# Attention scores from two full-height products a head, and all batches in half units

## The chip, the cores and the metric

The kernel runs on one core of a Trainium2 chip. Its engines work side by side, each on its own list of instructions in a fixed order: TensorE (PE, with its weight loads as PEld), VectorE (DVE), ScalarE (ACT), GpSimd (POOL), and SyncE (SP), which here issues all DMAs. Time is device microseconds (us) of one launch, the median of several runs; a profiled execution stands beside it.

## The reference

A small attention with a memory term feeds a two-layer network:

```python
scores = (q @ k.T) / sqrt(D)          # B, H, S, D = 4, 8, 576, 64, causal
local = softmax(scores) @ v
q_p = where(q > 0, q, exp(q) - 1) + 1
mem_out = (q_p @ M_prev) / (q_p @ z_prev + 1e-6)
x = g * mem_out + (1 - g) * local     # g = sigmoid(beta), per head
out = square(relu(x.reshape(2304, 512) @ w_in)) @ w_out     # 512 -> 2048 -> 512
```

All of it is fp32. Products that need more than TensorE's fast fp32 form (fp32r) holds are built from a high part, rounded to fp32r, and a low part, the remainder.

## The kernel before

The network's 2304 tokens go in nine blocks of 256. A block costs 192 `up` products of 256 columns (lines 624 to 626: four contraction slices by 16 slices of the hidden layer, three high/low terms each) and 96 `oacc` products of 512 columns (lines 614 to 616). Block 0 holds the first 64 tokens of the four batches. Each batch then gives two blocks: its query tiles 1 and 2 (the low half), and its tiles 3 and 4 (the high half). A block can start once all four head pairs of its batch have written their half of `x` to `xd` and `prefetch` has read it back as `xn` and transposed it into `px` (lines 588 and 591).

Attention goes in units (b, p, tiles): a batch, a pair of heads, and the query tiles worked on. `SEG = 2` makes half units of batches 0 and 1 (lo and hi, `[1, 2]` and `[3, 4]`) and whole units of batches 2 and 3, so 16 half units (0 to 15) and 8 whole ones (16 to 23). Units 0 to 5 (`NES`) use fp32 directly for the scores and are not split. From unit 6 on, q and k are split: `qh` and `kh` by ACT (lines 359 and 364), `ql` by DVE (line 360), `kl` by POOL in units below 12 (`NEARLY`) and by DVE from there (line 365). One DMA brings k (`kd`), one or two bring q with the memory matrix (`qm`), one brings v (`vv`); `kd` and `vv` have one buffer.

Scores of a tile stand at line 461. The two heads of a pair lie on partitions 0 to 63 and 64 to 127, so each product contracts over 64 rows. A pass is one stretch of keys of one query tile: three terms (high by high, low by high, high by low), each for both heads, six products. Tiles 1, 2 and 3 have one pass of 192, 320 and 448 columns, tile 4 has two of 288. Line 465 (DVE) takes each pass out of PSUM, and the one PSUM buffer `s` is free after that. ACT takes the exponential, `a` is formed in two 16-bit parts, a DMA transposes it into `aT`, and lines 541 to 546 multiply by v. Each unit also scales v once: a maximum over `vv` (line 393, DVE), a broadcast on TensorE (`vt`, line 397), four small DVE steps (lines 395 to 403), and two 16-bit parts (lines 408 on ACT, 410 on DVE).

The order on each engine is set by a scheduler that simulates the program: network products fill TensorE's list where attention, which has to wait for other engines, leaves room. Once made, an engine's order is fixed; an instruction that waits holds up all behind it on its engine.

Of the kernel before, what the change touches and what calls it, by code (L numbers as in the profile page):

```python
# [21 lines left out]
P = 128  # L22
# [37 lines left out]
NEARLY = 12  # L60
SEG = 2
TORD = [2, 1, 3, 4]
# [25 lines left out]
def fused_kernel(ctx: ExitStack, tc: tile.TileContext, t0_d, zt_d, kk_d, qv_d, beta, w_in, w_out, out):  # L88
# [32 lines left out]
    def gates():  # L121
# [10 lines left out]
        nc.vector.tensor_scalar(out=g1b, in0=gpb, scalar1=-1.0, scalar2=1.0, op0=ALU.mult, op1=ALU.add)  # L132

    mask0 = cp.tile([P, D], F32, name="mask0")
    nc.vector.tensor_copy(mask0[:D], mask[:D, 448 : 448 + D])
    nc.vector.tensor_copy(mask0[D:], mask[D:, 512 : 512 + D])

# [84 lines left out]
    def first_tokens(tp, ahead):  # L222
        me, ze, se, xe, ye = ([nc.gpsimd if c == "p" else nc.vector for c in t] for t in TE)
        xh = mo.tile([P, NK, BLK], F32R, tag="xh", name="xh", bufs=2)
        xl = mo.tile([P, NK, BLK], F32R, tag="xl", name="xl", bufs=2)
        xq.append((xh, xl))
        ng = B // GB
        bc = [P, GN, D]
# [4 lines left out]
        for step in SEQ.split():  # L233
            if step == "r":
                ahead()
            elif step == "l":
                nxt.append(loads(*order[0]))
            elif step == "g":
# [90 lines left out]

    def loads(b, p, tiles):  # L330
        qa, qb = QT[tiles[0]][0], sum(QT[tiles[-1]])
        kd = at.tile([P, S], F32, tag="kd", name="kd", bufs=KB)
        nc.sync.dma_start(kd[:, :qb], kk_d[b, p, :, :qb])
        qm = at.tile([P, 2 * ZW + SQ], F32, tag="qm", name="qm", bufs=QB)
        qa, qb = qa - D + 2 * ZW, qb - D + 2 * ZW
        for c0, c1 in [(0, qb)] if qa == 2 * ZW else [(0, 2 * ZW), (qa, qb)]:
            nc.sync.dma_start(qm[:, c0:c1], qv_d[b, p, :, c0:c1])
        vv = at.tile([P, 5 * P], F32, tag="vv", name="vv", bufs=VVB)
        nv = (tiles[-1] + 1) * P
        nc.sync.dma_start(vv[:, :nv], qv_d[b, p, :, SQ + 2 * ZW : SQ + 2 * ZW + nv])  # L340
        return kd, qm, vv

    def attention(b, p, tiles, ld, after, early, sfull, full):
# [5 lines left out]
        qa, qb = QT[tiles[0]][0] - D, kn - D  # L349
        kd, qm, vv = ld  # L350
        q_raw = qm[:, 2 * ZW :]
# [4 lines left out]
        if not sfull:  # L356
            qh, ql = (at.tile([P, SQ], F32R, tag=t, name=t) for t in ("qh", "ql"))
            kh, kl = (at.tile([P, S], F32R, tag=t, name=t) for t in ("kh", "kl"))
            nc.scalar.copy(qh[:, qa:qb], q_raw[:, qa:qb])
            q_eng.tensor_tensor(  # L360
                out=ql[:, qa:qb], in0=q_raw[:, qa:qb], in1=qh[:, qa:qb].bitcast(F32), op=ALU.subtract
            )
            yield
            nc.scalar.copy(kh[:, :kn], kd[:, :kn])
            k_eng.tensor_tensor(out=kl[:, :kn], in0=kd[:, :kn], in1=kh[:, :kn].bitcast(F32), op=ALU.subtract)
            yield
            terms = [(qh, kh), (ql, kh), (qh, kl)]
        else:
            terms = [(q_raw, kd)]

# [76 lines left out]
        for i in [t for t in TORD if t in tiles]:  # L447
# [8 lines left out]
            for s in range(ns):  # L456
                ks = slice(s * w, (s + 1) * w)
                sps = ps.tile([P, 2, 512], F32, tag="s", name="sp")
                for x, (qt, kt) in enumerate(terms):
                    for h, hd in enumerate(heads):  # L460
                        nc.tensor.matmul(  # L461
                            sps[:n, h, :w], qt[hd, qc], kt[hd, ks], start=x == 0, stop=x == len(terms) - 1
                        )
                for h in range(2):
# [236 lines left out]
    if not nxt:  # L701
        nxt.append(loads(*order[0]))

    def attn(i0, i1):
        for i in range(i0, i1):
            ld = nxt.pop()

            def after():
                if i + 1 < len(order):
                    nxt.append(loads(*order[i + 1]))  # L710

            yield from attention(*order[i], ld, after, i < NEARLY, i < NES, i < NEF and max(order[i][2]) < 4)
# [67 lines left out]
```

## Time and profile before

| | before |
|---|---|
| time, median of 3 runs | 610.11 us (610.11 to 610.82) |
| profiled execution | 609.23 us, of which the span is 607.4 us |
| PE busy | 569.1 us (94%) |
| DVE busy | 411.2 us (68%) |
| ACT busy | 329.0 us (54%) |
| POOL busy | 170.3 us (28%) |

The span runs from the first instruction to the last; 1.8 us of the execution lie outside it. A matmul's start in the trace is measured and its end modelled, so matmuls overlap in the list: what a product holds the engine for is read from the distance between starts. Attention ends at about 480 us; behind it only the network runs.

### The profile page before, as it was taken

To read this page: it belongs to the slowest core of one execution; us is meant where nothing else is said; L and a number is where in the kernel's file an instruction comes from. 1 tells how busy PE (TensorE), PEld (TensorE's weight loads), DVE (VectorE), ACT (ScalarE), POOL (GpSimd) and SP (SyncE) were. 2 spreads that over 40 slices of the span, in tenths; PEclk is the share of its full clock that TensorE was granted. 3 is DMA by queue.
4 is the path that set the end of the run, shared out by engine and by line. 5 is a ranking of instruction groups with operands and counts; after the bars stand their busy time and mean duration, and the time that the engine had idled before them with its cause. 6 is when DMAs were issued, how large, how long until landed. Compare 5 with 4: busy or idle time off the path is not lost.

```text
span 607.4 us, 11542 instructions
## 1 busy us (share of the span) xinstructions
PE 569.1 (94%) x4198; PEld 482.7 (79%) x4198; DVE 411.2 (68%) x1285; ACT 329.0 (54%) x747; POOL 170.3 (28%) x139
## 2 busy tenths in 40 slices
PE   2479997999989999999999999999999999999997
PEld 2358876787868787888888888888888899998996
DVE  5999798868677879887888978788697711001000
ACT  3689686756566664775576645654556413312312
POOL 2501232134423233233332233232321121221221
PEclk9989998999997999999999999999999999999999
DMA  8947575673574775664655564575435510100000
GB/s 278 402 144 301 165 210 159 139 169 85 117 165 111 160 155 129 145 173 88 164 115 114 145 126 107 114 167 118 103 70 119 99 24 2 68 1 1 36 1 35
DMA packets 127576, 76.28 MB, mean 126 GB/s; under 512 B 99360, under 2 KB 112672, under 8 KB 127520
## 3 DMA queue, kind: packets, MB, share of 16 engines
q1 hardware_dynamic: 127520, 75.55, 49.7%
q8 instruction: 33, 0.54, 0.4%
q14 instruction: 23, 0.19, 0.1%
HBM read 42.63 MB, written 8.78 MB: 85 GB/s over the span
## 4 chain that ended last, share of the span: by engine, by line
PE 63%; DVE 13%; DMA 9%; ACT 9%; issue 3%; SPq 1%; POOL 1%; ACTq 0%
PE up L624 9%; PE up L626 8%; PE up L625 8%; PE oacc L614 8%; PE oacc L616 8%; PE oacc L615 8%; PE sp L461 6%; DMA aT<-a 3%; DMA vv<-in_qv_dram 3%; ACT e L477 2%; PE acc L546 2%; DVE a L516 2%; PE pm L428 2%; DVE e L465 2%; DVE memx L556 2%
## 5 line engine op out<-in xcount | busy, mean ns | idle before, releaser
L624 PE MATMUL up<-xh,w 128*128 128x256 f32 x576 | 167.0, 290 | 3.4 <-ACT aF L496 2.5
L626 PE MATMUL up<-xh,w 128*128 128x256 f32 x576 | 166.1, 288 | 0.0
L625 PE MATMUL up<-xl,w 128*128 128x256 f32 x576 | 165.9, 288 | 0.0
L639 POOL TENSOR_TENSOR gl<-r,gh 128x512 fp32r<-128x512 f32 x72 | 98.9, 1373 | 203.6 <-DVE gh L638 124.4
L624 PEld LDWEIGHTS up<-xh,w 128*128 128x128 f32 x576 | 111.2, 193 | 10.9 <-issue 3.9
L614 PE MATMUL oacc<-w,gh 128*128 128x512 f32 x288 | 116.0, 403 | 3.6 <-ACT gh L636 3.5
L625 PEld LDWEIGHTS up<-xl,w 128*128 128x128 f32 x576 | 111.3, 193 | 5.2 <-issue 2.5
L615 PE MATMUL oacc<-w,gh 128*128 128x512 f32 x288 | 114.4, 397 | 0.0
L626 PEld LDWEIGHTS up<-xh,w 128*128 128x128 f32 x576 | 111.2, 193 | 3.4 <-issue 2.2
L477 ACT ACTIVATE e<-e,mx 128x320 f32<-128x320 f32 (+3 forms) x128 | 77.8, 609 | 65.4 <-DVE mx L465 65.0
L616 PE MATMUL oacc<-w,gl 128*128 128x512 f32 x288 | 111.7, 403 | 0.0
L516 DVE SCALAR_TENSOR_TENSOR a<-e,a 128x128 f16<-128x128 f32 x120 | 79.4, 677 | 19.8 <-ACT a L514 19.6
L630 ACT ACTIVATE r<-up 128x512 f32<-128x512 f32 x72 | 42.4, 590 | 92.5 <-PE up L626 86.6
L632 POOL TENSOR_TENSOR r<-r 128x512 f32<-128x512 f32 x40 | 46.5, 1162 | 164.1 <-ACT r L630 164.1
L638 DVE CAST gh<-r 128x512 fp32r<-128x512 f32 x40 | 16.9, 423 | 87.9 <-ACT r L634 86.4
L614 PEld LDWEIGHTS oacc<-w,gh 128*128 128x128 f32 x288 | 54.5, 189 | 15.7 <-ACT gh L636 4.0
L616 PEld LDWEIGHTS oacc<-w,gl 128*128 128x128 f32 x288 | 53.2, 189 | 13.5 <-issue 3.8
L465 DVE CUSTOM_DVE_ANT_0 e<-sp,mask 128x320 f32<-128x320 f32 (+3 forms) x128 | 56.2, 475 | 9.0 <-PE sp L461 8.9
L615 PEld LDWEIGHTS oacc<-w,gh 128*128 128x128 f32 x288 | 54.5, 189 | 9.4 <-issue 0.9
L514 ACT ACTIVATE a<-e 128x128 f16<-128x128 f32 x120 | 56.9, 521 | 5.7 <-DMA aT<-a 4.7
L548 DVE TENSOR_REDUCE s<-acc 128x128 f32<-128x256 f32 x60 | 24.0, 417 | 21.2 <-PE acc L546 21.2
L546 PE MATMUL acc<-vs,aT 128*128 128x128 f16 x308 | 37.4, 222 | 0.0
(127 smaller groups left out, 883.4 us busy)
## 6 DMA issues: line engine op xcount, KB each, us to landing
raw<-in_w_in_dram SPq DMA_DIRECT2D x11, 512.0 KB, 7.9
vv<-in_qv_dram SPq DMA_DIRECT2D x16, 320.0 KB, 2.8
raw<-in_w_out_dram SPq DMA_DIRECT2D x9, 512.0 KB, 7.8
kd<-in_kk_dram SPq DMA_DIRECT2D x16, 288.0 KB, 3.1
out_dram<-o SPq DMA_DIRECT2D x16, 256.0 KB, 2.0
xd<-memx SPq DMA_DIRECT2D x31, 128.0 KB, 2.1
xn<-xd SPq DMA_DIRECT2D x14, 256.0 KB, 3.2
qm<-in_qv_dram SPq DMA_DIRECT2D x8, 321.0 KB, 2.9
```

What stands on the lines that cost most here:

```text
L465: nc.vector.tensor_tensor_reduce(out=e[:n, h, ks], in0=sps[:n, h, :w], in1=mask[:n, 448 - q0 + s * w : 448 - q0 + s * w + w], scale=-0.125 ...
L477: nc.scalar.activation(e[:n, h, :ke], e[:n, h, :ke], AF.Exp, bias=bs, scale=-1.0, accum_out=sm[:n, h : h + 1])
L514: nc.scalar.mul(av[:, :, o0 : o0 + w], x, SC)
L516: nc.vector.scalar_tensor_tensor(out=av[:, :, o0 + w : o0 + 2 * w], in0=x, scalar=SC, in1=av[:, :, o0 : o0 + w], op0=ALU.mult, op1=ALU.sub ...
L546: nc.tensor.matmul(o2, aT[:, h * nb + c, :n], vs[:, h, c], start=False, stop=c == i)
L614: nc.tensor.matmul(acc[t], gh[:, u, ts], w_out_op(f, 0), start=f == 0, stop=False)
L615: nc.tensor.matmul(acc[t], gh[:, u, ts], w_out_op(f, 1), start=False, stop=False)
L616: nc.tensor.matmul(acc[t], gl[:, u, ts], w_out_op(f, 0), start=False, stop=f == NF - 1)
L624: nc.tensor.matmul(up[:, u, :], w_in_op(f, k, 0), xh[:, k, :], start=k == 0, stop=False)
L625: nc.tensor.matmul(up[:, u, :], w_in_op(f, k, 0), xl[:, k, :], start=False, stop=False)
L626: nc.tensor.matmul(up[:, u, :], w_in_op(f, k, 1), xh[:, k, :], start=False, stop=k == NK - 1)
L639: nc.gpsimd.tensor_tensor(out=gl, in0=r, in1=gh.bitcast(F32), op=ALU.subtract)
```

## The change

k's high and low part are stacked in one tile: rows 0 to 63 hold the high part of one head's k, rows 64 to 127 its low part, the two heads side by side. For that k is loaded onto both halves of the partitions, ACT rounds all of it, and the lower half is overwritten with the remainder. q is loaded onto both halves too, into a buffer `qd` of its own, and split there into `qh` and `ql`. A product of `qh` with that tile over 128 rows then gives high by high and high by low at once, and one of `ql` adds low by high (and low by low, which the kernel before leaves out). A pass is four products over 128 rows in place of six over 64. The new tiles have room for two query tiles, and `SEG = 4` makes half units of all batches: 32 units, with 16 to 19 and 24 to 27 the low halves of batches 2 and 3. The small `mask0` moves to a pool that is given back early.

```diff
-SEG = 2
+SEG = 4
...
+            kd = at.tile([P, 2, S], F32, tag="kd", name="kd", bufs=KB)
+            qd = at.tile([P, 2, 2 * P], F32, tag="qd", name="qd")
+            for r in range(2):
+                rs = slice(r * D, (r + 1) * D)
+                nc.sync.dma_start(kd[rs, :, :qb], kk_d[b, p, :, :qb].rearrange("(h d) s -> d h s", h=2))
+            q0 = qa - D + 2 * ZW
+            for r in range(2):
+                rs = slice(r * D, (r + 1) * D)
+                nc.sync.dma_start(
+                    qd[rs, :, : qb - qa], qv_d[b, p, :, q0 : q0 + qb - qa].rearrange("(h d) s -> d h s", h=2)
+                )
...
-            qh, ql = (at.tile([P, SQ], F32R, tag=t, name=t) for t in ("qh", "ql"))
-            kh, kl = (at.tile([P, S], F32R, tag=t, name=t) for t in ("kh", "kl"))
-            nc.scalar.copy(qh[:, qa:qb], q_raw[:, qa:qb])
+            qn = qb - qa
+            qh, ql = (at.tile([P, 2, 2 * P], F32R, tag=t, name=t) for t in ("qh", "ql"))
+            kh = at.tile([P, 2, S], F32R, tag="kh", name="kh")
+            kf, lo = kh.bitcast(F32), slice(D, P)
+            nc.scalar.copy(kh[:, :, :kn], kd[:, :, :kn])
+            k_eng.tensor_tensor(out=kh[lo, :, :kn], in0=kd[lo, :, :kn], in1=kf[lo, :, :kn], op=ALU.subtract)
+            yield
+            nc.scalar.copy(qh[:, :, :qn], qd[:, :, :qn])
             q_eng.tensor_tensor(
-                out=ql[:, qa:qb], in0=q_raw[:, qa:qb], in1=qh[:, qa:qb].bitcast(F32), op=ALU.subtract
-            )
-            yield
-            nc.scalar.copy(kh[:, :kn], kd[:, :kn])
-            k_eng.tensor_tensor(out=kl[:, :kn], in0=kd[:, :kn], in1=kh[:, :kn].bitcast(F32), op=ALU.subtract)
-            yield
-            terms = [(qh, kh), (ql, kh), (qh, kl)]
-        else:
-            terms = [(q_raw, kd)]
+                out=ql[:, :, :qn], in0=qd[:, :, :qn], in1=qh.bitcast(F32)[:, :, :qn], op=ALU.subtract
+            )
+            yield
...
-                for x, (qt, kt) in enumerate(terms):
-                    for h, hd in enumerate(heads):
-                        nc.tensor.matmul(
-                            sps[:n, h, :w], qt[hd, qc], kt[hd, ks], start=x == 0, stop=x == len(terms) - 1
-                        )
+                for h, hd in enumerate(heads):
+                    if sfull:
+                        nc.tensor.matmul(sps[:n, h, :w], q_raw[hd, qc], kd[hd, ks], start=True, stop=True)
+                        continue
+                    qs = slice(qc.start - qa, qc.stop - qa)
+                    nc.tensor.matmul(sps[:n, h, :w], qh[:, h, qs], kh[:, h, ks], start=True, stop=False)
+                    nc.tensor.matmul(sps[:n, h, :w], ql[:, h, qs], kh[:, h, ks], start=False, stop=True)
```

Lines move with the change: the score products are at 477 and 478 after it, the k split at 375 and 376, the q split at 378 and 379, the `up` products at 639 to 641, the `oacc` products at 629 to 631, `px` at 606.

On TensorE, the last score pass of the program (tile 4 of the last head pair of batch 3) with the network's products around it stands before the change as

```order
L616 MATMUL oacc<-w_104,gl 128x512
L614 MATMUL oacc<-w_104,gh 128x512
L461 MATMUL sp<-kh,qh 128x288 x2
L461 MATMUL sp<-kh,ql 128x288 x2
L461 MATMUL sp<-kl,qh 128x288 x2
L615 MATMUL oacc<-w_104,gh 128x512
L616 MATMUL oacc<-w_104,gl 128x512
```

and after it as

```order
L630 MATMUL oacc<-w_99,gh 128x512
L631 MATMUL oacc<-w_99,gl 128x512
L477 MATMUL sp<-kh,qh 128x288
L478 MATMUL sp<-kh,ql 128x288
L477 MATMUL sp<-kh,qh 128x288
L478 MATMUL sp<-kh,ql 128x288
L629 MATMUL oacc<-w_99,gh 128x512
L630 MATMUL oacc<-w_99,gh 128x512
```

The pass has four products in place of six, and it stands later: 1224 `up` and 592 `oacc` products are ahead of it before, 1392 and 675 after.

On TensorE again, between the network's block 1 (the low half of batch 0, whose last products are `oacc` of `w_1156`) and block 2 (`px` is its input): before the change the scores of unit 9 stand in and behind the last products of block 1,

```order
L461 MATMUL sp<-kh,qh 128x320 x2
L461 MATMUL sp<-kh,ql 128x320 x2
L616 MATMUL oacc<-w_1011,gl 128x512 x2
...
L614 MATMUL oacc<-w_1156,gh 128x512
...
L461 MATMUL sp<-kl,qh 128x320 x2
...
L461 MATMUL sp<-kh,qh 128x192 x2
...
L591 MATMUL px<-identr,xn 128x128 x8
```

and after the change all passes of units 8 and 9 stand behind block 1:

```order
L477 MATMUL sp<-kh,qh 128x288
L478 MATMUL sp<-kh,ql 128x288
L441 MATMUL pm<-qm 128x130 x2
...
L631 MATMUL oacc<-w_1156,gl 128x512
...
L477 MATMUL sp<-kh,qh 128x320
...
L477 MATMUL sp<-kh,qh 128x192
...
L606 MATMUL px<-identr,xn 128x128 x8
```

The pass of 288 columns at the head of the second list is the last one of unit 7, the last high half of batch 0. Network products that stood behind it have moved ahead of it: of block 1, 37 `up` and 36 `oacc` products stand between it and `px` before, and 12 `oacc` products after.

On DVE, the preparation of unit 16, the first one of batch 2, is before the change

```order
L365 TENSOR_TENSOR kl<-kd,kh 128x576
L360 TENSOR_TENSOR ql<-qm,qh 128x512
L393 TENSOR_REDUCE vx<-vv 128x1
...
L395 TENSOR_SCALAR vx<-vx 128x1
...
L377 SCALAR_TENSOR_TENSOR qm<-pe,qm 128x512
```

and after it, for the low half alone (the high half does it all again as unit 20, with 64x1152 for k),

```order
L379 TENSOR_TENSOR ql<-qd,qh 128x512
...
L376 TENSOR_TENSOR kh<-kd,kh 64x2x320
...
L406 TENSOR_REDUCE vx<-vv 128x1
...
L408 TENSOR_SCALAR vx<-vx 128x1
...
L390 SCALAR_TENSOR_TENSOR qm<-pe,qm 128x256
```

A (batch, head pair) of batches 2 and 3 now has two such preparations on DVE where it had one.

## Rows read from the trace of the kernel before

**Rows 1.** Windows: us, busy time and instructions per engine, granted clock, DMA share, GB/s

```profile
0.00:120.00 120.00, 91.97 (x639) 74.80 (x640) 106.11 (x307) 85.17 (x198) 29.03 (x29) 0.96 0.71 225
120.00:180.00 60.00, 56.42 (x450) 46.88 (x448) 44.75 (x145) 35.28 (x82) 24.25 (x19) 1.00 0.62 134
180.00:240.00 60.00, 57.85 (x416) 48.05 (x417) 48.36 (x180) 38.30 (x96) 18.31 (x15) 0.94 0.66 141
260.00:480.00 220.00, 219.09 (x1717) 184.07 (x1716) 179.60 (x572) 126.02 (x293) 64.77 (x51) 1.00 0.54 119
480.00:607.00 127.00, 123.80 (x817) 112.27 (x815) 14.97 (x35) 32.82 (x56) 27.14 (x21) 1.00 0.10 29
```

**Rows 2.** Timeline of PE, a 192-column pass: start us, duration us, instruction, idle before

```profile
200.25 0.28 PE L625 MATMUL up<-xl,w 128*128 128x256 f32 x1
200.45 0.36 PE L461 MATMUL sp<-kh,qh 64*128 64x192 f32 x2
...
200.97 0.39 PE L626 MATMUL up<-xh,w 128*128 128x256 f32 x1
```

**Rows 3.** Timeline of PE, a 288-column pass and 512-column products before it

```profile
287.19 0.39 PE L615 MATMUL oacc<-w,gh 128*128 128x512 f32 x1
...
289.00 0.39 PE L614 MATMUL oacc<-w,gh 128*128 128x512 f32 x1
289.32 0.40 PE L461 MATMUL sp<-kh,qh 64*128 64x288 f32 x2
...
289.92 0.50 PE L615 MATMUL oacc<-w,gh 128*128 128x512 f32 x1
```

**Rows 4.** Timeline of PE, a 320-column pass cut in two

```profile
298.16 0.28 PE L625 MATMUL up<-xl,w 128*128 128x256 f32 x1
298.28 0.28 PE L626 MATMUL up<-xh,w 128*128 128x256 f32 x1
298.49 0.41 PE L461 MATMUL sp<-kh,qh 64*128 64x320 f32 x2
298.83 0.23 PE L541 MATMUL acc<-vs,aT 128*128 128x128 f16 x1
...
299.41 0.22 PE L546 MATMUL acc<-vs,aT 128*128 128x128 f16 x1
299.56 0.41 PE L461 MATMUL sp<-kh,ql 64*128 64x320 f32 x2
...
300.05 0.39 PE L624 MATMUL up<-xh,w 128*128 128x256 f32 x1
```

**Rows 5.** Timeline of PE, a 448-column pass

```profile
385.25 0.28 PE L626 MATMUL up<-xh,w 128*128 128x256 f32 x1
385.46 0.47 PE L461 MATMUL sp<-kh,qh 64*128 64x448 f32 x2
...
386.26 0.50 PE L614 MATMUL oacc<-w,gh 128*128 128x512 f32 x1
```

**Rows 6.** Groups by line and shape: count, busy us, mean ns of one

```profile
L410 DVE SCALAR_TENSOR_TENSOR vs<-vv,vy,vs 128x192 f16<-128x192 f32 x12 | 4.5, 413 | 0.0
L365 DVE TENSOR_TENSOR kl<-kd,kh 128x576 fp32r<-128x576 f32 x12 | 9.0, 750 | 0.0
L360 DVE TENSOR_TENSOR ql<-qm,qh 128x512 fp32r<-128x512 f32 x8 | 7.4, 925 | 0.0
L398 DVE TENSOR_REDUCE vy<-vt 128x1 f32<-128x128 f32 x22 | 6.2, 281 | 0.0
L365 POOL TENSOR_TENSOR kl<-kd,kh 128x576 fp32r<-128x576 f32 x2 | 3.7, 1834 | 7.3 <-ACT kh L364 7.3
L393 DVE TENSOR_REDUCE vx<-vv 128x1 f32<-128x384 f32 x6 | 3.3, 549 | 1.8 <-DMA vv<-in_qv_dram 1.8
```

**Rows 7.** Timeline of PE, unit 7's last pass and block 2's first transposes

```profile
158.24 0.52 PE L461 MATMUL sp<-kl,qh 64*128 64x288 f32 x2
...
180.80 1.35 PE L591 MATMUL px<-identr,xn 128*128 128x128 f32 x8 [2.10 <-DMA xn<-xd]
```

## What the change will do to the time

> **What bounds the kernel now.** I read the windows first. From 260 to 480 us TensorE shows 219.09 us of work in 220, at a granted clock of 1.00 (all of 2.4 GHz), while DVE shows 179.60 (82%) and ACT 126.02 (57%) [rows 1]. Behind 480 us only the network is left, and TensorE is again the busy one. So from about the middle of the span on, the end is set by how many microseconds of product TensorE has to stream, and a microsecond taken off TensorE's list there is one off the time, as long as nobody else falls behind. Before that it is different: in 120 to 180 and 180 to 240 us TensorE is busy 56.42 and 57.85 of 60 us [rows 1], and the longest wait is in the timeline: the transposes of block 2 stand idle 2.10 us for `xn`, which comes out of the attention of batch 0 [rows 7]. Ahead of that point the pace is shared between TensorE's fixed order and attention's chain through ACT, DVE and DMA.
>
> Next I looked at what a score pass costs, by distance between starts. Plain products give the scale: the two of 256 columns at 298.16 and 298.28 start 0.12 us apart [rows 4], and eight of 512 columns take the 1.81 us from 287.19 to 289.00, 0.226 each, so 0.44 ns a column [rows 3]. What a pass takes is the distance from the product ahead of it to the one behind it, less that first product's own slot:
> - 192 columns: 200.97 - 200.25 - 0.12 = 0.60 us [rows 2]
> - 288: 289.92 - 289.00 - 0.23 = 0.69 [rows 3]
> - 448: 386.26 - 385.25 - 0.12 = 0.89 [rows 5]
> - 320, cut in two by products with v: 298.83 - 298.28 - 0.12 = 0.43, and 300.05 - 299.41 - 0.04 (the last product with v) = 0.60, together 1.03 [rows 4].
>
> The columns alone don't explain this. The two heads of a term sit in one row "x2" of 0.36 us, hardly longer than one product, so they run side by side and a pass streams three times its width: 3 x 192 x 0.44 ns = 0.25 us of the 0.60, and 0.38 of the 0.69. The other 0.3 us is paid at the edges: the first 64-row product starts 0.20 us behind a 256-column product that needs 0.12 [rows 2], and what follows the last one starts late too. A pass cut in two pays it twice.
>
> The page TensorEngine Tiling (Array Packing) of the Trainium skill says under Tiling Modes, Key Properties, that a change of tiling mode drains the engine; by that, full-height products would pay nothing at the edges, and the 0.3 us that the rows show agree with it.
>
> **The change part by part.** *Passes.* From unit 6 on there are 66 passes. Those up to block 2's transposes (units 6 to 9, ten passes) fall into the stretch that TensorE does not set alone. The other 56, from unit 10 on, are 24 of 288, 12 of 448, 10 of 320 and 10 of 192. In the order before, all ten of 320 are cut in two, five of 448, three of 288 and one of 192; I price a cut at 0.3 more. Before: 24 x 0.69 + 3 x 0.3 = 17.5; 12 x 0.89 + 5 x 0.3 = 12.2; 10 x 1.03 = 10.3; 10 x 0.60 + 0.3 = 6.3; together 46.3 us. After: four full-height products a pass, like the network's own, at 0.44 ns a column: 0.51, 0.79 and 0.56 us for 288, 448 and 320. For 192 columns each product costs between 0.085 (columns) and 0.12 (what 256 columns take); I take 0.10, so 0.40. Sum: 12.2 + 9.5 + 5.6 + 4.0 = 31.3 us. TensorE saves 15 us. If the edges stay whatever the height, four widths against three make it 9 us more instead (one width more in each of the 66 passes, 20,480 columns x 0.44 ns); if a cut costs nothing before, the saving is 12.
>
> *Eight more units.* TensorE gets eight more `vt`, 0.1 us each by the distances between such starts: +0.8. DVE gets more. Of k, 64 rows by 1152 columns replace 128 by 576 at 750 ns [rows 6]. The bounds are 750 (the same number of elements) and 1500 (twice the columns); I take 1350, since DVE's other rows grow with columns (413 ns for 192, 750 for 576). A low half has 640 columns, about 820. `ql` has 512 columns in every half unit, 925 ns a time [rows 6]. For one (batch, head pair) of batches 2 and 3 that is 1.35 + 0.82 - 0.75 for k, 0.92 for q, 0.55 for one more maximum over `vv`, 0.83 for two more low parts of v, and about 1.0 for five small steps of which the longest is 0.28 [rows 6]: 4.7 us, of which I count 4.4 because the add behind the relu gets cheaper in two halves. Eight times: 35 us on DVE. ACT gets about 30 us over the span by the same doubling of columns, and with 126 of 220 it has the room.
>
> Does DVE have it? The order answers with room in time: the last pass now stands behind 1392 `up` and 675 `oacc` products where it had 1224 and 592, by 0.12 and 0.226 us 39 us more network ahead of it. So the stretch of batches 2 and 3, 220 us before, becomes 220 - 11 (its 40 passes' share of the saving) + 39 = 248 us, and DVE has 179.6 + 35 + 4 (its part of that network work) = 219 us to do in it: 88% where it had 82%. In the first 120 us DVE was busy 106.11 of 120, 88% [rows 1], so it can be had. I put +3 us on TensorE for waits behind DVE, with 0 and 20 as ends (the latter in the rivals). Blocks 3 to 8 are not starved by it: in the order, at least 18 us of products lie between the last pass that each needs and its transposes.
>
> *Loads.* k comes twice and q twice more: by shapes some 16 MB on 75 MB. DMA was busy 0.54 to 0.66 in these stretches [rows 1] and SP issues some 60 more. They go out a unit ahead, and q no longer waits for `qm`. Hidden: 0; if a transposing DMA is held up by 0.5 us in a unit, the slack in front of the products with v covers it.
>
> *The start.* Before, 37 `up` and 36 `oacc` products of block 1 stand between unit 7's last pass and block 2's transposes, 12.6 us by the distances above; now 12 `oacc`, 2.7 us. So TensorE has 9.9 us more to do ahead of unit 7's last pass, at 158.24 [rows 7]. Less the idle time that it had there (some 2 us) and 1.5 us saved on the six passes of units 6 and 7, that pass comes at about 164 to 165. From there to the transposes it was 180.80 - 158.24 = 22.6 us [rows 7], mostly attention's own chain, with POOL's k split now some 1.8 us longer (twice 1834 ns less what was [rows 6]); with fewer products in between I take 20. Block 2 then starts at 185, 4 us late, and behind it the list of network products is as long as before. Ends: 4 us early (the ten early passes save that, if attention follows), 9 us late.
>
> **The sum.** Span 607.4 - 15 + 0.8 + 4 + 3 = 600.2. The profiled execution was 609.23, 1.8 over its span, and the median of the runs is 0.9 above that: 603.
>
> **The rivals.**
> 1. *Nothing is given back.* Block 2 starts no later and DVE keeps up: 610.1 - 15 + 0.8 - 4 = 592. For it: TensorE hardly waited for DVE before. Against it: the order between unit 7 and block 2.
> 2. *DVE takes the bound in batches 2 and 3*, slower. The place is the in-order list of DVE with two preparations a (batch, head pair). If it can't be filled above the 82% that it had, 219 us of work need 268 us in place of 248, +20 in place of the +3: 620. The deciding point: 7 us over the forecast's 251 the change has lost its gain, at 219 / 258 = 85%. For it: 120 to 180 us, where TensorE waited now and then, shows DVE at 75% [rows 1]. Against it: 88% in the first 120 us.
> 3. *The height doesn't pay.* The side-by-side heads are lost and the edges stay: 610.1 + 9 + 0.8 + 4 + 3 = 627. For it: the "x2" rows, against it: edges are seen only at 64-row products; where a full-height product follows another of other shape (298.83 on) starts stay at the columns [rows 4].
>
> The same page, Overview, promises up to twice the speed to contractions of at most 64 rows when they are packed, which is what this change gives up; by that alone rival 3 would hold. The rows show its gain (two heads in the time of one) and a larger price.
>
> 4. *The start costs all*: two more starved stretches of 5 us like block 2's, 610 to 613. For it only the thin order there.
>
> **How the numbers follow.** Forecast 603: 0.50. Rival 1: 0.22. Rival 2: 0.17, mostly between 610 and 621. Rival 3: 0.05. Rival 4: 0.06. What a measurement can tell from no change is about 0.2%, 1.2 us. Faster: 0.22 + 0.48 of the forecast's 0.50 = 0.70. The same: 0.02 of the forecast, 0.02 of rival 2, 0.02 of rival 4, together 0.06. Slower: the rest, 0.24. The forecast's own range is 597 to 608; with rival 1 and the near part of rival 2 the range is 591 to 616.
>
> **What would show it.** Right: score products of 288 columns 0.13 us apart with no wider step at either edge; block 2's transposes at about 185 us; DVE close to 90% in batches 2 and 3 with TensorE near 100% there. Wrong on passes: steps of 0.2 us at their edges. Rival 2 would show as idle time of TensorE in front of score products, released by line 480 of DVE, and as a last pass later than 505 us. The forecast fails most easily on the DVE term, which is the difference of two large numbers.

## The result: slower by 0.8%

| | before | after |
|---|---|---|
| time, median | 610.47 us (610.11 to 610.91) | 615.17 us (614.4 to 616.98) |
| ratio to before | | 1.0081, 95% interval 1.0055 to 1.0107 |
| profiled execution, span | 609.23, 607.4 us | 616.98, 615.2 us |
| TensorE busy, not busy | 569.1, 38.3 us | 555.9, 59.3 us |

The forecast was 603 us, faster. That 615 us lies just inside its range, 591 to 616, is owed to the part added for rival 2 and says nothing for its sum. TensorE did get less to do, by 13.2 us, but stood idle 21.0 us longer. The passes did what the forecast says. The timeline of PE after the change, a pass of 192 columns, one of 288 (the last of unit 7), one of 320 and one of 448, each with its neighbours:

```profile
302.10 0.25 PE L477 MATMUL sp<-kh,qh 128*128 128x192 f32 x1
302.19 0.28 PE L478 MATMUL sp<-kh,ql 128*128 128x192 f32 x1
302.30 0.28 PE L477 MATMUL sp<-kh,qh 128*128 128x192 f32 x1
302.41 0.27 PE L478 MATMUL sp<-kh,ql 128*128 128x192 f32 x1
302.53 0.30 PE L641 MATMUL up<-xh,w 128*128 128x256 f32 x1
...
167.94 0.39 PE L631 MATMUL oacc<-w,gl 128*128 128x512 f32 x1
168.17 0.29 PE L477 MATMUL sp<-kh,qh 128*128 128x288 f32 x1
...
168.70 0.61 PE L441 MATMUL pm<-qm 128*128 128x130 f32 x4
...
327.35 0.31 PE L477 MATMUL sp<-kh,qh 128*128 128x320 f32 x1
...
327.94 0.28 PE L639 MATMUL up<-xh,w 128*128 128x256 f32 x1
...
157.90 0.37 PE L477 MATMUL sp<-kh,qh 128*128 128x448 f32 x1
...
158.71 0.28 PE L639 MATMUL up<-xh,w 128*128 128x256 f32 x1
```

From the first score product to the start of what follows, these are 0.43, 0.53, 0.59 and 0.81 us, against 0.60, 0.69, 1.03 and 0.89 before [rows 2 to 5]. Behind a 512-column product the first score product starts 0.23 us later, which is that product's own slot: no step is left at the edges.

The windows show where the time went (columns as in [rows 1]):

```profile
0.00:120.00 120.00, 88.22 (x609) 70.62 (x609) 104.03 (x296) 84.24 (x194) 31.27 (x28) 0.96 0.71 223
120.00:180.00 60.00, 54.27 (x415) 47.72 (x411) 41.22 (x127) 35.53 (x73) 28.05 (x19) 0.98 0.67 146
180.00:240.00 60.00, 51.24 (x372) 46.64 (x372) 46.19 (x149) 36.02 (x91) 18.25 (x15) 0.88 0.65 147
260.00:480.00 220.00, 214.63 (x1635) 194.88 (x1634) 191.81 (x596) 137.28 (x318) 72.64 (x53) 0.99 0.71 161
480.00:607.00 127.00, 124.87 (x896) 113.45 (x895) 51.73 (x152) 49.93 (x95) 26.80 (x20) 1.00 0.31 71
```

TensorE lost 3.8 us of work in the first 120, 2.2 in 120 to 180, 6.6 in 180 to 240 and 4.5 in 260 to 480. The stretch from 180 to 240 us is the worst. Its granted clock of 0.88 is a mean over both levels, 1.2 and 2.4 GHz: 0.67 in 180 to 190 us, 0.63 in 190 to 200, 1.00 from 200 on. It was 1.00 in 150 to 170 us and fell behind the idle time of these rows (timeline of PE after, its longer waits up to block 2):

```profile
176.77 0.36 PE L477 MATMUL sp<-kh,qh 128*128 128x192 f32 x1 [3.46 <-DVE mx L480]
180.89 0.29 PE L556 MATMUL acc<-vs,aT 128*128 128x128 f16 x1 [3.16 <-DMA aT<-a]
185.42 0.36 PE L477 MATMUL sp<-kh,qh 128*128 128x192 f32 x1 [1.07 <-DVE mx L480]
187.37 0.27 PE L556 MATMUL acc<-vs,aT 128*128 128x128 f16 x1 [1.25 <-DVE vs L423]
191.06 0.75 PE L606 MATMUL px<-identr,xn 128*128 128x128 f32 x4 [2.15 <-DMA xn<-xd]
```

Block 2 starts at 191.06 where it was 180.80 [rows 7]; block 1's first transposes come at 110.99 (102.93 before). From block 2 to the end of the span it is 424.1 us, 426.6 before. So of the 7.8 us of span 8.1 are lost by block 1, 2.2 from there to block 2, and only 2.5 are won back behind it, where the forecast has 11 to win. Behind block 2 TensorE waits for several engines (waits of PE after, from 196 us on; total, times, longest; four groups of 0.2 to 0.6 us left out):

```profile
PE acc L556 <- DMA aT<-a: 2.6, 5, 1.1
PE vt L410 <- DVE vx L408: 2.2, 2, 1.7
PE sp L477 <- DVE kh L376: 2.1, 2, 1.6
PE px L606 <- DMA xn<-xd: 1.5, 2, 1.3
PE acc L556 <- DVE vs L423: 1.3, 2, 0.7
```

With the groups left out these are 11.4 us. Before, the whole list has 1.9:

```profile
PE acc L541 <- DMA aT<-a: 0.8, 1, 0.8
PE sp L461 <- DVE mx L465: 0.7, 1, 0.7
PE sp L461 <- ACT qh L359: 0.4, 1, 0.4
```

### The profile page after: what moved, and what is told of

It reads as the page before. It is cut to its first block, busy times and chain, and to the rows that moved or that the text cites. A ratio compares the mean times of both kernels' runs of the same rounds, so it can differ in the third digit from the quotient of the medians.

```text
span 615.2 us, 11620 instructions
## 1 busy us (share of the span) xinstructions
PE 555.9 (90%) x4074; PEld 492.4 (80%) x4074; DVE 450.1 (73%) x1373; ACT 353.8 (58%) x787; POOL 183.2 (30%) x139
## 4 chain that ended last, share of the span: by engine, by line
PE 39%; DVE 24%; DMA 19%; ACT 8%; issue 6%; POOL 2%; SPq 1%; ACTq 0%; DVEq 0%; POOLq 0%
DMA vv<-in_qv_dram 7%; DMA aT<-a 6%; PE up L639 6%; PE up L640 6%; PE up L641 6%; PE oacc L629 5%; PE oacc L630 5%; PE oacc L631 5%; DVE a L531 3%; DVE e L480 2%; DMA raw<-in_w_in_dram 2%; DVE kh L376 2%; DVE memx L571 2%; ACT e L492 2%; DVE s L563 2%
## 5 line engine op out<-in xcount | busy, mean ns | idle before, releaser
L654 POOL TENSOR_TENSOR gl<-r,gh 128x512 fp32r<-128x512 f32 x72 | 103.5, 1437 | 218.6 <-DVE gh L653 116.2
L631 PE MATMUL oacc<-w,gl 128*128 128x512 f32 x288 | 109.4, 396 | 1.4 <-POOL gl L654 1.4
L531 DVE SCALAR_TENSOR_TENSOR a<-e,a 128x128 f16<-128x128 f32 x120 | 73.6, 628 | 20.8 <-ACT a L529 20.5
L647 POOL TENSOR_TENSOR r<-r 128x512 f32<-128x512 f32 x40 | 48.4, 1209 | 119.2 <-ACT r L645 112.5
L477 PE MATMUL sp<-kh,qh 128*128 128x288 f32 (+3 forms) x132 | 42.4, 333 | 6.7 <-DVE mx L480 4.5
L478 PE MATMUL sp<-kh,ql 128*128 128x288 f32 (+3 forms) x132 | 41.1, 323 | 0.0
```

The costliest lines, as they stand in the source:

```text
L531: nc.vector.scalar_tensor_tensor(out=av[:, :, o0 + w : o0 + 2 * w], in0=x, scalar=SC, in1=av[:, :, o0 : o0 + w], op0=ALU.mult, op1=ALU.sub ...
L631: nc.tensor.matmul(acc[t], gl[:, u, ts], w_out_op(f, 0), start=False, stop=f == NF - 1)
L647: nc.gpsimd.tensor_tensor(out=r, in0=r, in1=r, op=ALU.mult)
L654: nc.gpsimd.tensor_tensor(out=gl, in0=r, in1=gh.bitcast(F32), op=ALU.subtract)
```

## Experiments

Every kernel's order is planned anew, so a run says what an edit does together with the order that follows from it. "Block 1", "block 2" and "rest" are from the profiled execution: the first transposes of the two blocks, and from block 2's to the span's end; it can lie some us from the median (e17: span 609.4, median 614.75). The runs e1, e6, e8, e9, e10, e13 and e14 mix the two heads or use one of them, so they don't compute the reference; the others do. Where a run's name is followed by that of another kernel, as in "e7 e5", it is that kernel with the edit named.

| run | time, us | ratio to before (95%) | block 1 | block 2 | rest |
|---|---|---|---|---|---|
| before | 609.5 to 610.9 | | 102.9 | 180.8 | 426.6 |
| after | 615.17 | 1.0081 (1.0055 to 1.0107) | 111.0 | 191.1 | 424.1 |
| e1 tall products alone | 596.07 | 0.9750 (0.9718 to 0.9783) | 104.1 | 178.9 | 414.9 |
| e2 half units alone | 620.26 | 1.0151 (1.0119 to 1.0183) | 102.7 | 181.6 | 435.9 |
| e3 after, whole units in batches 2, 3 | 624.21 | 1.0220 (1.0184 to 1.0257) | 110.8 | 190.1 | 430.1 |
| e4 after, k's low part on GpSimd | 633.83 | 1.0371 (1.0315 to 1.0426) | 112.4 | 192.3 | 438.3 |
| e5 after, q in k's buffer | 622.93 | 1.0196 (1.0165 to 1.0227) | 103.7 | 188.8 | 433.5 |
| e6 tall products and half units | 597.41 | 0.9772 (0.9742 to 0.9801) | 103.6 | 178.2 | 418.9 |
| e7 e5, k loaded once | 627.67 | 1.0282 (1.0261 to 1.0303) | 103.9 | 184.5 | 442.0 |
| e8 new loads, old splits | 622.76 | 1.0205 (1.0175 to 1.0234) | 101.6 | 194.2 | 426.1 |
| e9 old loads, new splits | 612.78 | 1.0037 (1.0020 to 1.0054) | 103.7 | 184.7 | 426.7 |
| e10 e9, two buffers for `kh` | 610.97 | 1.0005 (0.9981 to 1.0030) | 103.9 | 185.8 | 423.7 |
| e11 e7, two buffers for `kh` | 619.50 | 1.0148 (1.0111 to 1.0186) | 102.8 | 181.5 | 435.8 |
| e12 before, two buffers for `kh`, `kl` | 606.62 | 0.9938 (0.9918 to 0.9958) | 103.8 | 182.5 | 422.9 |
| e13 e9, k's low part on DVE only | 615.94 | 1.0094 (1.0065 to 1.0123) | 103.3 | 186.4 | 427.0 |
| e14 e9, units 6 and 7 unsplit | 602.80 | 0.9881 (0.9851 to 0.9911) | 102.5 | 178.8 | 421.5 |
| e15 e11, units 6 and 7 unsplit | 626.40 | 1.0256 (1.0226 to 1.0286) | 104.4 | 185.9 | 439.5 |
| e16 after, units 6 and 7 unsplit | 627.30 | 1.0289 (1.0274 to 1.0304) | 110.5 | 187.1 | 438.6 |
| e17 e5, units 6 and 7 unsplit | 614.75 | 1.0084 (1.0046 to 1.0122) | 102.6 | 180.2 | 429.2 |
| e18 before, units 6 and 7 unsplit | 604.48 | 0.9907 (0.9888 to 0.9927) | 103.8 | 182.5 | 421.1 |

**The parts alone: e1, e2, e6.** The first has the tall products on the old tiles, the second the half units, the third both.

```diff
-                for x, (qt, kt) in enumerate(terms):
-                    for h, hd in enumerate(heads):
-                        nc.tensor.matmul(
-                            sps[:n, h, :w], qt[hd, qc], kt[hd, ks], start=x == 0, stop=x == len(terms) - 1
-                        )
+                for h, hd in enumerate(heads):
...
+                    nc.tensor.matmul(sps[:n, h, :w], qh[:, qc], kh[:, ks], start=True, stop=False)
+                    nc.tensor.matmul(sps[:n, h, :w], ql[:, qc], kl[:, ks], start=False, stop=True)
```

> The kernel before with the shape of the score products alone changed: four products of 128 rows a pass on the tiles that it has (so the scores mix the two heads and are not attention's; loads, splits, units and everything behind are as before). Theory: the product shape is worth what the trace after shows, 0.53 us for a pass of 288 columns where it was 0.69, about 14 us behind block 2 and up to 20 in all, and the loss comes with the preparation: 592 to 598 us. Rival: the scheduler's order for full-height products itself costs the start, so block 1 and block 2 begin late here too (block 1's transposes at 108 us or later in place of 103): 600 to 608.

> The kernel before with half units for all batches and nothing else: eight more preparations of v and k, about 2.4 us of DVE each, products and loads as before. If the extra units are what holds TensorE up in batches 2 and 3: 613 to 617 us, with idle time of TensorE behind block 2 that the kernel before does not show. If they are hidden under the network's products: 609 to 612.

> The kernel before with both the four 128-row products a pass (on its old tiles of k and q, which mixes the two heads: the scores are not the reference's) and half units of all batches, and with the loads and splits of the kernel before. With the two single runs it makes a square: passes alone gave 596.1, half units alone 620.3, before 610.8. Theory A (the two add): 596.1 + 9.5 = 605.6, so 604 to 607, and the 9 to 10 us up to the kernel after (615.2) are the price of the stacked loads and splits. Theory B (half units cost more once TensorE's passes are shorter, since DVE and the transposing DMAs then set the pace): 609 to 615, and the stacked loads and splits would cost little. Theory C (half units cost less with shorter passes, since TensorE's extra time in them was edges of passes): 598 to 603.

e1 came out as expected, e2 dearer than both theories, and e6 by its theory C or a little below it: half units cost 9.5 us on the old passes and 1.3, within the intervals, on tall ones. e6 has everything of the kernel after but the stacked loads and splits, so these, with the order that follows from them, cost 615.2 - 597.4 = 18 us. Busy time of the engines (page of e6):

```profile
PE 549.4 (92%) x4074; PEld 490.6 (82%) x4074; DVE 431.6 (72%) x1373; ACT 337.0 (56%) x787; POOL 167.4 (28%) x139
```

The same number of products as after, 4074, in 6.5 us less, and 11.6 us less idle time. The 6.5 us go with the granted clock: over the span it was 0.983 in e6 and 0.974 after, and 549.4 x 0.983 and 555.9 x 0.974 are nearly the same, 540 and 541 us. The 18 us are 13 by block 2 and 5 behind it.

**Guesses on the kernel after: e3, e4.** e3 makes the units of batches 2 and 3 whole again and splits their q in two goes; e4 sets `LATE = 'dp'`, which gives k's low part to GpSimd from unit 12 on.

> The changed kernel with whole units in batches 2 and 3 again: k stacked as a whole, q split in two goes inside the unit, so the full-height products stay and the second preparation of v and k goes (4.4 us more DVE work a head pair become about 1.5). If DVE's extra work behind block 2 is the cause of the idle time there (9 us): 604 to 608 us, the start as late as in the changed kernel. If most of the loss is the start alone: 611 to 615. If both theories are off and the loads are the cause (DMA share 0.73 where it was 0.55): between, with vv still waited for.

> The changed kernel with the low part of k formed on POOL in units 12 to 31 too: DVE loses some 23 us of work, POOL gets 20 instructions of 1.6 to 2.7 us. If DVE's load behind block 2 is the cause: idle time of TensorE there falls by half, 609 to 612 us. If it is the length of the chain from load to scores, not the load: POOL's split is 1.3 us longer than DVE's, 615 to 620.

Both lost. e4 says that a slower engine on k's split costs more than a relieved DVE gives back. e3 is outside all that was expected: its block 4 lasts 84.6 us where the kernel after has 63.3. At the end of that block, from 384 to 398 us, TensorE waits 8.9 us, half of it for one transposing DMA, and its granted clock in 390 to 398 us is 0.50. What makes them come late there is not shown. Timeline of PE in e3:

```profile
391.72 0.29 PE L566 MATMUL acc<-vs,aT 128*128 128x128 f16 x1 [4.44 <-DMA aT<-a]
```

**The late start: e5 and e7.**

```diff
-            kd = at.tile([P, 2, S], F32, tag="kd", name="kd", bufs=KB)
-            qd = at.tile([P, 2, 2 * P], F32, tag="qd", name="qd")
+            kq = at.tile([P, 2, S + 2 * P], F32, tag="kd", name="kd", bufs=KB)
+            kd, qd = kq[:, :, :S], kq[:, :, S:]
```

> The kernel after, but q is loaded into the tail of k's buffer in place of a buffer of its own; nothing else. In the order, SyncE's first loads then stand as in the kernel before, and q of units 6 and 7 no longer goes out among the weights. Theory A (the 8 us by which block 1's transposes come late, 111.0 against 102.9 us, come from those early loads of q, which shift the loads and splits of the weights): block 1's transposes come back to about 103 us, and the time falls by most of 8 us, to 606 to 609. Theory B (the late start would be taken up by waits for DVE and for transposing DMAs further on, which set the end whatever the start): block 1 at 103 us, but time 612 to 616. Theory C (the late start has another cause, for example ScalarE's and DVE's doubled splits): block 1 stays at 109 to 111 us and the time at 614 to 617.

> The kernel after with q in the tail of k's buffer, and with k loaded once over 128 partitions as in the kernel before: ScalarE and DVE (or GpSimd) then build the stacked tile, each in two instructions of 64 rows, one a head, with the low part written to the other half of the partitions. The same columns on each engine as the kernel after, some 8 MB less to load. Theory A (the start is cured, and the rest of the loss is DVE's and the half units'): 606 to 609, like the run with q in k's buffer alone. Theory B (the second copy of k costs, by DMA queues that hold up aT and vv behind block 2): 3 to 6 us below that run, 601 to 605. Theory C (two instructions in place of one, on an engine that is short of time): 1 to 3 us above that run.

In e5 theory A is right on block 1, and all three miss the time. Block 1 is back at 103.70, so in this kernel its 8 us depend on q's own buffer, free from the beginning: the loads for units 6 and 7 go out among the weights, the first two at 20.90 us. But block 2 wins only 2.3 us of the 8, and the time is 8 us longer than that of the kernel after. Timeline of SyncE after (`SPq` is its queue), then of PE in e5, the two transposes:

```profile
20.90 1.90 SPq L345 DMA_DIRECT2D qd<-in_qv_dram  x2
```

```profile
103.70 0.54 PE L606 MATMUL px<-identr,xn 128*128 128x128 f32 x3
...
188.76 0.75 PE L606 MATMUL px<-identr,xn 128*128 128x128 f32 x4 [1.14 <-DMA xn<-xd]
```

In e7 loading k once, with twice the instructions to split it, was 4.7 us slower than e5 (theory C, and more), although block 2 came 4.3 us earlier.

**Loads or splits: e8, e9.** e8 splits `kd[:, 0]` and `qd[:, 0]` as before; e9 reads the columns twice:

```diff
-            nc.scalar.copy(kh[:, :, :kn], kd[:, :, :kn])
+            kd2 = kd[:, None, :kn].to_broadcast([P, 2, kn])
+            nc.scalar.copy(kh[:, :, :kn], kd2)
...
```

> The kernel after (615.2) with its loads of k and q, each twice, but with the splits of the kernel before on 128 partitions, half as many columns (only the first head's columns are used, so the scores are not the reference's). Four 128-row products a pass and half units as after. Against the run that has tall products and half units with the old loads and splits (597.4) it adds the loads alone; 18 us lie between that run and the kernel after. Theory A (the loads cost it: q's own buffer takes the weight stage apart, 8 us, and the doubled traffic holds up aT and vv): 608 to 615. Theory B (the doubled splits cost it, on DVE, GpSimd and ScalarE): 597 to 602. Theory C (half each, the late start from the loads and the rest from the splits): 604 to 608.

> The kernel after (615.2) with its stacked tiles and doubled splits, instruction for instruction, but with the loads of the kernel before: k and q come once, and the splits read the same columns twice (so the heads are mixed and the scores are not the reference's). Theory A (the loads cost the 18 us): 597 to 602, with block 1's transposes at 103 us. Theory B (the doubled splits cost them): 609 to 616, although block 1 is at 103 us. Theory C (half each): 604 to 608.

Each alone costs about as much as the two together, or more: 25 and 15 us over e6, against 18. e9 came out by its theory B; e8 is slower than all three of its theories. e8 has its loss by block 2 (194.2) and behind it, and not at the start: q goes out among the weights as in the kernel after, yet block 1 is on time. So the early loads alone don't make block 1 late; only the runs that have them together with the doubled splits are late (after, e3, e4 and e16, 110.5 to 112.4 us). Timelines of SyncE and PE in e8:

```profile
20.93 1.83 SPq L345 DMA_DIRECT2D qd<-in_qv_dram  x2
```

```profile
101.59 0.45 PE L605 MATMUL px<-identr,xn 128*128 128x128 f32 x3
```

Half of e8's loss is not idle time. Its span is 23.2 us over that of e6, of which 11.5 are idle time and 11.7 the same number of products at a lower granted clock (0.961 over the span; 561.1 x 0.961 is 539 us, nearly what e6 has). Busy time of the engines (page of e8):

```profile
PE 561.1 (90%) x4074; PEld 497.6 (80%) x4074; DVE 426.8 (69%) x1373; ACT 339.6 (55%) x787; POOL 170.6 (28%) x139
```

Waits of PE from 196 us on, in e8, then in e9 and in e6:

```profile
PE acc L555 <- DMA aT<-a: 11.2, 6, 3.8
```

```profile
PE acc L550 <- DMA aT<-a: 4.4, 7, 1.6
```

```profile
PE acc L542 <- DMA aT<-a: 4.7, 4, 2.3
```

With the new loads TensorE mostly waits longer for the transposing DMAs: 11.2 us in e8, 11.8 in e5, 12.7 in e16, 10.4 in e17. But the kernel after has 2.6, and e14 below, with the old loads, has 7.9 and is 10 us faster than e9 with 4.4, so these waits alone don't rank the runs.

**Are the splits in series with the units? e10, e11, e12.**

```diff
-            kh = at.tile([P, 2, S], F32R, tag="kh", name="kh")
+            kh = at.tile([P, 2, S], F32R, tag="kh", name="kh", bufs=2)
```

> The run with the doubled splits and the old loads (612.8; the heads are mixed), with a second buffer for the stacked k tile, so that the next unit's k can be split while the scores of this one still read theirs; every instruction stays. Theory A (the splits stand in series with the units: in the traces the k split of a unit starts 1.6 us behind the last score pass of the unit before where it started 1.0 us behind it, and the first pass of a unit comes 7.05 us behind it where it came 6.1 with the old splits; TensorE starves on that): with the split off that path the gap from a unit's last pass to the next unit's first falls to 5.5 to 6 us, TensorE's idle time falls by 6 to 10 us, and the time to 601 to 607. Theory B (it is the busy time of DVE, ScalarE and GpSimd that is too long, wherever the split stands): 611 to 615.

> The run with k loaded once and stacked on the chip (627.7), with a second buffer for the stacked k tile; qm is cut to two query tiles to make room for it, and every instruction stays. It computes the reference. Theory A (the splits stand in series with the units): as in the run beside it, 8 to 12 us less, 615 to 620, and the gap from a unit's last pass to the next unit's first falls from 7.2 to about 6 us. Theory B (busy time of the engines that split): 625 to 629.

> The kernel before with a second buffer for kh and kl; nothing else. Theory A (the units' series sets the pace only where TensorE runs short of products; before, TensorE was busy 99.6% of 260 to 480 us): 607 to 611, a few us at most from the stretch up to block 2. Theory B (splitting ahead is worth the same everywhere): 598 to 604.

In e10 the gap between units (DVE's last read of one unit's scores to its first of the next, mean) fell from 7.05 to 6.49 us over units 16 to 31, about half of what theory A has, and the last score product started at 501 us, not 518. The time fell by 1.8 us, which is within the intervals, where theory A has 6 to 12: it is wrong for this kernel. In e11 it holds: the gap fell from 7.23 to 6.21 us and 8 us came back. In e12 3.5 came back, about as theory A has it.

**The splits ahead of block 2: e13, e14.** e13 sets `EARLY = 'dd'`, which gives k's low part to DVE below unit 12 too; e14 sets `NES = 8`, which leaves units 6 and 7 unsplit.

> The run with the doubled splits and the old loads (612.8, block 2's first transposes at 184.7 us; the heads are mixed), with the low part of k made by DVE in all units, where GpSimd made it in units 6 to 11. Theory A (GpSimd's 2.7 us a unit stand in the chain to block 2): block 2 at 181 to 183 us, time 609 to 611. Theory B (DVE is as short of time there as GpSimd is slow): block 2 at 184 to 187, time 612 to 615.

> The run with the doubled splits and the old loads (612.8; the heads are mixed), with units 6 and 7 left unsplit like units 0 to 5 (fp32 products on 64 rows, two a pass), so that no split stands ahead of block 2. Theory A (the loss ahead of block 2 comes from the splits of units 6 and 7, and is carried to the end): block 2 at 178 to 181 us where it was 184.7, time 606 to 609. Theory B (it is carried, but the unsplit passes cost as much on TensorE as the splits): block 2 at 182 to 185, time 610 to 613. Theory C (the start is won back and lost again behind block 2, where attention sets the pace): block 2 at 178 to 181, time 611 to 614.

Taking the work from GpSimd doesn't help (e13, theory B). Without the splits of units 6 and 7 block 2 comes 5.9 us earlier, about where e6 has it, and the time is 10 us shorter, more than expected. Timeline of PE, block 2's first transposes in e9, then in e14:

```profile
184.68 0.75 PE L600 MATMUL px<-identr,xn 128*128 128x128 f32 x4 [1.24 <-DMA xn<-xd]
```

```profile
178.82 1.50 PE L600 MATMUL px<-identr,xn 128*128 128x128 f32 x8 [0.37 <-DMA xn<-xd]
```

**Does the cure carry over? e15 to e18.** All four set `NES = 8`.

> The run with k loaded once, stacked on the chip, and two buffers for the stacked tile (619.5, block 2 at 181.5 us), with units 6 and 7 left unsplit as well. It computes the reference. Theory A (what is won ahead of block 2 is carried to the end): block 2 at 178 to 180 us, time 615 to 617. Theory B (behind block 2 this kernel is paced by attention): time 618 to 621. Either way it stays above the kernel before (610).

> The kernel after (615.2; block 1 at 111.0, block 2 at 191.1 us) with units 6 and 7 left unsplit, nothing else. In the order, q of units 8 and 9 now goes out among the weights in place of q of units 6 and 7. Theory A (the stacked splits ahead of block 2 cost 6 us there and about 10 in all, as in the run with the old loads): block 2 at 184 to 186 us, time 604 to 608; a start before 105 us would add to it. Theory B (with the doubled loads the stretch stays starved, whatever the splits): block 2 at 189 or later, time 612 to 617.

> The run with q in the tail of k's buffer (622.9; block 1 at 103.7, block 2 at 188.8 us) with units 6 and 7 left unsplit. Theory A (splits ahead of block 2): block 2 at 181 to 183 us, time 611 to 615. Theory B (doubled loads): block 2 at 187 or later, time 620 to 624.

> The kernel before (610.3; block 2 at 180.8 us) with units 6 and 7 left unsplit. Theory A (its splits are short and its passes of six products for these units cost about what the unsplit ones do): block 2 at 179 to 181 us, time 608 to 611. Theory B (leaving two units unsplit is worth as much in any of these kernels): block 2 at 175 us, time 599 to 604.

With e5's loads it does (e17, theory A: block 2 8.6 us earlier, 8 us less). On the kernel after it does not, and e16 is 10 us slower than the upper end of what was expected: block 2 comes 4 us earlier, but the rest takes 438.6 us where it took 424.1, with these waits (PE in e16, from 196 us on):

```profile
PE acc L556 <- DMA aT<-a: 12.7, 9, 2.6
PE vt L410 <- DVE s L563: 2.1, 3, 1.2
PE up L639 <- DVE xl L612: 1.9, 2, 1.1
```

e15 lost 7 us, ahead of block 2 and behind it, where a gain or nothing was expected. e18 shows that the kernel before gains 5 us from it too, more than theory A has, but not by an earlier block 2 (182.5). So what e14 gains ahead of block 2 is the price of the stacked splits there. e18, at 604.5 us, is the fastest kernel here that computes the reference, and it does not have the change.

## Why the prediction was wrong

The forecast's span is 600.2 us and the measured one 615.2. The 15.0 us between them lie in three terms of its sum:

| term | forecast | measured |
|---|---|---|
| passes | -15 | -13.7, estimated from one measured slot of each width |
| start of block 2 | +4 | +10.3 |
| waits behind block 2 (DVE +3, loads 0) | +3 | +10.4, what the other terms leave of the 7.8 us; the lists of waits have 11.4 - 1.9 = 9.5 |
| eight more `vt` | +0.8 | taken as forecast |

The second and the third failed.

**The passes: right.** For the 56 passes behind block 2 the measured slots give 24 x 0.53 + 12 x 0.81 + 10 x 0.59 + 10 x 0.43 = 32.6 us, for 31.3 forecast: a saving of 13.7 in place of 15. e1 shows that it reaches the time where loads, splits and units stay: 610.8 - 596.1 = 14.7 us, early passes included. The Trainium skill (TensorEngine Tiling (Array Packing), Tiling Modes), cited there, says that a change of tiling mode drains the engine. The trace agrees: the step at the edges of 64-row passes, 0.3 us a pass, is gone with products of full height.

**The start: the step that failed first.** The forecast has block 2 4 us late; it came 10.3 late. Unit 7's last pass came at 168.17 us, not 164 to 165, and from there to block 2 it took 191.06 - 168.17 = 22.9 us, as before the change, and not 20. The forecast worked from the list between blocks 1 and 2 and took block 1 as unmoved; block 1 came 8.1 us late. How much of that reaches block 2 is not shown: with block 1 on time e5 wins 2.3 us there. The longer split it counted only as GpSimd's 1.8 us. GpSimd's was 0.8 longer (2664 for 1834 ns), but taking the splits of units 6 and 7 away brought block 2 forward by 5.9 us in e14 and by 4.0 in e16, where the kernel before wins nothing by it (e18).

**"Hidden: 0" for the loads: wrong.** e8 has nothing new but these loads over e6, and the order that follows, and is 25 us slower. They were priced by their bytes against a DMA share of 0.54 to 0.66; the room was there (0.71 in 260 to 480), but k landed later, SyncE had more to issue in one queue with the transposing DMAs, and the order moved. Which of these it was is not separated. The forecast also reckoned with some 60 more issues. SyncE has 110 more, 364 for 254: 34 of `kd`, 52 of `qd`, 24 of `qm` and `vv` for the eight more units. DMA issues of `qd` after the change (count, KB each, median us from issue to landing):

```profile
qd<-in_qv_dram SPq DMA_DIRECT2D x52, 128.0 KB, 2.9
```

**The splits and half units: busy time right, its effect not.** DVE's rows came out near the estimates (groups by form after the change):

```profile
L379 DVE TENSOR_TENSOR ql<-qd,qh 128x512 fp32r<-128x512 f32 x26 | 20.3, 782 | 0.5 <-ACT qh L378 0.5
L376 DVE TENSOR_TENSOR kh<-kd,kh 64x1152 fp32r<-64x1152 f32 x12 | 17.0, 1416 | 0.4
L376 DVE TENSOR_TENSOR kh<-kd,kh 64x640 fp32r<-64x640 f32 x8 | 6.6, 822 | 0.2
L376 POOL TENSOR_TENSOR kh<-kd,kh 64x1152 fp32r<-64x1152 f32 x2 | 5.3, 2664 | 5.0 <-issue 3.0 <-ACT kh L375 1.9
```

1416 and 822 ns for k, where 1350 and 820 were taken, 782 for `ql`, where 925 was taken, and 191.81 of 220 us busy, 87%, where 88% was forecast. Waits of 3 us were put on that. Behind block 2 the forecast wins 15 - 0.8 - 3 = 11.2 us; 2.5 came, with the passes only 1.3 short, so some 7 more were lost there. The waits named above put 5.6 us on DVE (`vx`, `kh`, `vs`) and 4.1 on DMAs.

**The rivals.** The waits for DVE are rival 2's mechanism, with 5.6 of its 20 us, and its range, 610 to 621, holds the measured time. Of its two signs one came, a last score pass later than 505 us (its first product starts at 524.58). But e9 has its last score product at 518 us and e8 at 500, and e8 is the slower one, so this sign alone tells little. The other, waits for line 480 in front of score products, shows only ahead of block 2 (3.46 and 1.07 us above). Rival 4 (610 to 613) was right in kind on a dearer start and 2 us short. Rival 3 is refuted by the slots. Timeline of PE after, the last score pass:

```profile
524.58 0.29 PE L477 MATMUL sp<-kh,qh 128*128 128x288 f32 x1
```

**What stays open.** That the stacked preparation costs more than the passes save holds in more than one order: the nine kernels that compute the reference from stacked tiles (after, e3, e4, e5, e7, e11, e15, e16, e17) took 614.8 to 633.8 us, the two with tall products and the old preparation (e1, e6) 596.1 and 597.4. But the 18 us of loads and splits don't divide: alone they cost 25 and 15. Cures that work in one kernel fail in another (e14 against e16, e11 against e10), with a rest of 419 to 442 us for the same number of products. Since each edit brings a new order on all engines, which of its places decide was not found; a run with a fixed order and one edit in it was not tried.

## What to carry to other kernels

A saving on the busiest engine counts only as far as the preparation that pays for it stays off the way to the next stage: ask first where the engine already waits (here block 2's input) and what the change puts in front of that. A load into a buffer of its own is not free because it can go early: it goes early, and can displace what was there. Where a planner sets the order, test the parts in a square (with and without each), since single parts need not add: here loads and splits cost 25 and 15 us alone and 18 together.

## What the runs showed of the hardware

An element-wise fp32 subtraction on 64 rows was not cheaper for its half height: 64x1152 took DVE 1416 ns where 128x576, as many elements, took 750, and GpSimd 2664 ns for 1834 [rows 6].

SyncE took nearly twice as long to issue a load that writes two heads side by side on 64 rows: 0.6 us for 0.33. Timeline of SyncE in e6, one load of k, then after the change two of k:

```profile
158.98 0.33 SPq L333 DMA_DIRECT2D kd<-in_kk_dram  x1
```

```profile
173.66 1.25 SPq L341 DMA_DIRECT2D kd<-in_kk_dram  x2
```

Each of the two loads of k has 288 KB, like the one before, and landed later; e8, with the same loads, has 4.2 us too, and e6, with the old ones, 3.1. DMA issues after the change, then before (count, KB each, median us from issue to landing):

```profile
kd<-in_kk_dram SPq DMA_DIRECT2D x30, 288.0 KB, 4.2
```

```profile
kd<-in_kk_dram SPq DMA_DIRECT2D x16, 288.0 KB, 3.1
```
